# Experts sorted by count on the chip, narrower blocks by rank, and some steps of the first half put elsewhere

## The chip, the cores and the metric

The kernel runs on one core of a Trainium2 chip. The metric is the device time of one execution in microseconds (us): 286.27 us is the median of three runs (285.29, 286.27 and 289.05). The engines are named as in the profile: PE (TensorE matmul; PEld is its weight load), DVE (VectorE), ACT (ScalarE), POOL (GpSimd) and SP (SyncE, which here only issues DMAs). An engine works through its own instructions in the order in which they stand, and waits at the first one whose inputs are not there.

## The reference

Two computations follow each other. The first is a state-space scan (Mamba-2 SSD) over 4 batches, 8 heads, 768 positions, head size 32 and state size 16. The second takes its output as 3072 tokens of width 256 and gives each token to one of 8 experts:

```
logits = xn @ en.T / tau                  # xn, en: tokens and expert embeddings, normalised
expert_idx = argmax(logits, axis=1)       # one expert for a token
gate_w = softmax(logits)[token, expert_idx]
for e in range(8):
    mask = expert_idx == e
    h = maximum(x[mask] @ w1[e], 0)       # 256 -> 1024
    out[mask] = gate_w[mask] * (h @ w2[e])  # 1024 -> 256
```

How many tokens each expert gets follows from the data. The reference, worked through with its own inputs, gives experts 0 to 7 the counts 408, 348, 366, 396, 382, 354, 405 and 413. Of expert 0's tokens 271 lie in the first four of the six position chunks.

## The kernel before, in words

**First half, `mamba`.** The 768 positions are cut into six chunks of 128, and each chunk into two pairs of batches, which makes twelve steps `s`. For a step PE computes `scores` (L493, into the PSUM tiles pgA and pgB), ACT copies them out (g, L509) and POOL masks them (L510; DVE masks some, L507), then PE makes `outputs` (L525 from the passed state T, L534 from the masked scores g and the scaled input xs) in the tile py. ACT copies py to yT (`keep_outputs`, L544), PE turns yT into tokens with their router logits (`tokens`, L583, in the tile pz), and ACT copies these to yt (`keep_tokens`, L594), from where SP writes them to a table `rows` in DRAM (L595). On odd steps PE also makes the chunk's `sums` (L552, in pz) from which DVE updates the state (V, L567, then T, L572). In odd steps V stands on DVE behind ACT's copy yt, since both read the tile pz.

Beside this runs the routing: DVE picks the expert of each token (`pick`, L346 to L355), PE counts ranks (`ranks`, L370), DVE turns a rank into a place in a table (`places`, `one_hots`: oh L386, low L415, hi L420, hv L424; ACT adds its part, hv L430) and PE scatters it there (`table`, L437; DVE adds it up in acc, L446). Decay factors are worked out on DVE; `spread_decays` (PE, L251) and `keep_decays` (ACT, fr, L258) spread them over partitions, `turn_inverse` (PE L239, ACT rT L240) transposes their inverses. All of this is in the order in which the code is written, engine by engine; nothing reorders it.

**Second half, `moe`.** Work is cut into nine jobs. Job 0 is the first 256 tokens of expert 0, which are known before the last chunks are through; job 1 is the rest of expert 0 in a block of 160; jobs 2 to 8 are experts 1 to 7 in blocks of 416. A job gathers its rows from DRAM (POOL, indirect DMA, L765), one DMA for each part of up to 128 rows; 416 is made of 128, 128, 128 and 32. PE transposes the parts (`turn_x`, L808; DVE copies xT, L810), multiplies by w1 (`up`, L818, eight slices f; ACT applies the Relu for even f, L822, DVE for odd f, L824), multiplies by w2 (`down`, L833, two slices j; ACT copies yoT for j = 0, L837, DVE for j = 1, L839) and transposes back (`out`, L847), then ACT and DVE scale by the gate (L853, L851) and POOL scatters the rows to the output (L854), again one indirect DMA a part. The gates come from ACT (squares, L776), POOL (a power, L780) and DVE (L786 to L798). A block is as wide as it is whatever the count, so rows beyond the count are computed for nothing.

Weights of expert 0 come in pieces during `mamba`; those of the other experts are two DMAs of 1 MB each from SP (`load_all_weights`, L181 for w1 and L182 for w2), into three buffers in turn. Experts 1 and 2 are requested before the routing table is complete, since their order is fixed.

If an expert has more than 416 tokens (`CAP`), `left_blocks` (spread over the jobs on DVE) counts the blocks that are left, and `leftover` at the end runs a loop over them: first 24 indirect DMAs of token numbers, then for each block weights, a gather, a whole job and a scatter. Each engine reads the number of blocks into a register (L1025) and skips this if it is zero.

## Time and profile before

| what | value |
|---|---|
| median of the runs (three) | 286.27 us |
| the profiled execution | 287.74 us, its span 286.0 us |
| busy: PE, DVE, ACT, POOL | 259.7, 119.3, 82.1, 102.3 us |
| end of `mamba`, first transposes of job 0 | 74.4 us after the span's start |
| jobs 4 to 7, from one `down` to the next | 24.9 us each |
| granted TensorE clock, mean | 0.98 |

The span is the time from the first to the last instruction of the profiled execution; about 1.7 us lie outside it. The profiled execution is 1.47 us above the median. Starts of instructions are counted from the span's start.

### The profile page before, as it was taken

What the parts mean: (1) busy time and instruction counts of PE and PEld (TensorE: products, weight loads), DVE (VectorE), ACT (ScalarE), POOL (GpSimd) and SP (SyncE); (2) the same over time, 40 slices, a digit from 0 to 9 for tenths busy, and PEclk for the clock granted to TensorE, in tenths of its full rate; (3) what the DMA queues carried; (4) which work ended last, traced back from release to release, by engine and by line L of the source; (5) the groups of instructions that cost most, each with busy time, mean ns of one, the idle gap of its engine ahead of it and who ended that gap; (6) DMA issues with size and microseconds to landing.
All of it is one profiled execution on the core that took longest, in us unless ns stands there. A gap on an engine that the chain in (4) does not pass through costs nothing.

```text
span 286.0 us, 5609 instructions
## 1 busy us (share of the span) xinstructions
PE 259.7 (91%) x2177; PEld 170.1 (59%) x2177; DVE 119.3 (42%) x376; ACT 82.1 (29%) x210; POOL 102.3 (36%) x124
## 2 busy tenths in 40 slices
PE   7698888859998999997999999999999999999980
PEld 6477677747787975554555555555555555555540
DVE  8875888964652431214304223330512323051140
ACT  3644655551421232032122103212220321222130
POOL 7724224443035263055107404710740470114024
PEclk9999999986999999999999999999999999999996
DMA  5656575840597361416224340622530020001001
GB/s 168 213 186 225 184 256 165 256 123 22 192 374 229 123 216 69 147 33 209 54 109 144 112 147 20 219 76 91 157 105 2 19 87 5 0 2 58 0 1 65
DMA packets 21342, 34.79 MB, mean 122 GB/s; under 512 B 2888, under 2 KB 14356, under 8 KB 21312
## 3 DMA queue, kind: packets, MB, share of 16 engines
q1 hardware_dynamic: 18272, 27.94, 29.3%
q0 software_dynamic: 2816, 6.40, 7.2%
q8 instruction: 18, 0.29, 0.4%
q14 instruction: 12, 0.10, 0.1%
q10 hardware_dynamic: 224, 0.06, 0.1%
HBM read 28.26 MB, written 6.65 MB: 122 GB/s over the span
## 4 chain that ended last, share of the span: by engine, by line
PE 52%; issue 22%; DVE 13%; POOL 7%; ACT 4%; POOLq 1%; DVEq 0%
PE bank L818 21%; PE bank L833 20%; POOL out_dram L854 3%; DVE low L415 3%; PE bank L808 2%; PE pz L583 2%; POOL xg L765 2%; PE py L534 2%; PE bank L847 1%; ACT yt L594 1%; PE py L525 1%; POOL g L510 1%; PE pgA L493 1%; ACT yo L853 1%; ACT g L509 1%
## 5 line engine op out<-in xcount | busy, mean ns | idle before, releaser
L818 PE MATMUL bank<-xT,w 128*128 128x416 f32 (+2 forms) x288 | 93.2, 475 | 1.2 <-DVE xT L810 0.8
L833 PE MATMUL bank<-hT,w 128*128 128x416 f32 (+2 forms) x288 | 91.7, 476 | 0.0
L833 PEld LDWEIGHTS bank<-hT,w 128*128 128x128 f32 x288 | 52.5, 190 | 34.9 <-issue 33.7
L818 PEld LDWEIGHTS bank<-xT,w 128*128 128x128 f32 x288 | 52.1, 190 | 35.4 <-issue 32.1
L824 DVE TENSOR_SCALAR hT<-bank 128x416 f32<-128x416 f32 (+2 forms) x33 | 18.3, 553 | 61.4 <-PE bank L818 59.1
L780 POOL TENSOR_TENSOR gr<-gr,half 128x4 f32<-128x4 f32 (+1 forms) x9 | 8.8, 975 | 94.1 <-ACT sq L776 94.1
L854 POOL DMA_INDIRECT out_dram<-yo,to x30 | 29.3, 977 | 23.1 <-ACT yo L853 15.3
L765 POOL DMA_INDIRECT xg<-rows,table x30 | 30.5, 1018 | 19.4 <-DVE to_u L465 11.2
L822 ACT ACTIVATE hT<-bank 128x416 f32<-128x416 f32 (+2 forms) x39 | 18.1, 470 | 62.7 <-PE bank L818 62.7
L510 POOL TENSOR_SCALAR_AFFINE_SELECT g<-g 128x1024 f32<-128x1024 f32 x16 | 18.1, 1144 | 31.5 <-ACT g L509 31.5
L791 DVE TENSOR_SCALAR gr<-gr 128x4 f32<-128x4 f32 (+1 forms) x9 | 1.5, 169 | 59.7 <-POOL gr L780 59.7
L837 ACT COPY yoT<-bank 128x416 f32<-128x416 f32 (+2 forms) x9 | 4.2, 468 | 61.1 <-PE bank L833 61.1
L493 PE MATMUL pgA<-cp,bz 32*128 32x128 f32 x192 | 13.9, 283 | 2.6 <-DVE cp L281 1.4
L534 PE MATMUL py<-g,xs 128*32 128x128 f32 x384 | 15.1, 288 | 0.4 <-issue 0.4
L509 ACT COPY g<-pgB 128x1024 f32<-128x1024 f32 x12 | 12.2, 1017 | 10.2 <-PE pgB L493 7.4
L583 PE MATMUL pz<-turn,yT 128*128 128x136 f32 x88 | 13.9, 304 | 0.9 <-ACT turn L339 0.6
L493 PE MATMUL pgB<-cp,bz 32*128 32x128 f32 x192 | 13.9, 283 | 0.0
L493 PEld LDWEIGHTS pgA<-cp,bz 32*128 32x128 f32 x192 | 11.6, 186 | 3.8 <-DVE cp L281 1.8
L583 PEld LDWEIGHTS pz<-turn,yT 128*128 128x128 f32 x88 | 11.7, 201 | 2.4 <-ACT turn L339 0.7
L534 PEld LDWEIGHTS py<-g,xs 128*32 128x32 f32 x384 | 10.8, 114 | 3.7 <-issue 2.3
L776 ACT ACTIVATE sq<-xg 128x256 f32<-128x256 f32 x32 | 12.9, 408 | 0.0
L847 PE MATMUL bank<-ident,yoT 128*128 128x128 f32 (+1 forms) x64 | 10.1, 276 | 2.9 <-DVE yoT L839 2.0
(200 smaller groups left out, 251.0 us busy)
## 6 DMA issues: line engine op xcount, KB each, us to landing
w<-in_moe_w_dram SPq DMA_DIRECT2D x14, 1024.0 KB, 5.0
rows<-yt SPq DMA_DIRECT2D x12, 264.0 KB, 3.6
in_x<-in_x_dram SPq DMA_DIRECT2D x6, 512.0 KB, 4.8
w<-in_moe_w_dram SPq DMA_DIRECT2D x8, 256.0 KB, 4.3
in_c<-in_CT_dram SPq DMA_DIRECT2D x6, 256.0 KB, 4.2
in_t<-in_B_dram SPq DMA_DIRECT2D x6, 256.0 KB, 5.7
bz<-in_BT_dram SPq DMA_DIRECT2D x40, 32.0 KB, 3.0
xg<-rows,table POOLq DMA_INDIRECT x30
```

The lines of the kernel that those rows point to most:

```text
L493: k.nc.tensor.matmul((k.pgA, k.pgB)[q // 2][:, q % 2, a : a + 128], lhsT=t.bz[r, v, b + i, :], rhs=t.cp[r, b + i, :], start=True, stop=Tru ...
L509: nc.scalar.copy(out=g, in_=ps)
L510: nc.gpsimd.affine_select(out=g, in_=g, pattern=[[0, 8], [1, Q]], compare_op=ALU.is_ge, fill=0.0, base=0, channel_multiplier=-1)
L534: nc.tensor.matmul(k.py[g : g + 32, v, 128 * i : 128 * i + 128], lhsT=t.xs[:, b + i, 4 * v + q, :], rhs=s.g[:, q, 2 * i + v, :], start=(c ...
L583: k.nc.tensor.matmul(at_[:, i, at : at + Y1], lhsT=yT[:, j, i, :], rhs=k.turn[:, j, :], start=(j == 0), stop=(j == 1), skip_group_check=True,)
L765: s.k.nc.gpsimd.indirect_dma_start(out=s.x[0:p, i, 0:TOK], out_offset=None, in_=rows, in_offset=bass.IndirectOffsetOnAxis(ap=s.at[0:p, i : ...
L818: nc.tensor.matmul(t, lhsT=s.w1[:, j, 128 * f : 128 * f + 128], rhs=s.xT[:, j, :], start=(j == 0), stop=(j == KD - 1))
L822: nc.scalar.activation(s.hT[:, f, :], t, ACT.Relu)
L824: nc.vector.tensor_scalar_max(s.hT[:, f, :], t, 0.0)
L833: nc.tensor.matmul(t, lhsT=s.w2[:, f, 128 * j : 128 * j + 128], rhs=s.hT[:, f, :], start=(f == 0), stop=(f == KF - 1))
L847: nc.tensor.transpose(t[:p, 128 * j : 128 * j + 128], s.yT[:, j, o : o + p], k.ident[:])
L854: d = nc.gpsimd.indirect_dma_start(out=k.out[:, :], out_offset=bass.IndirectOffsetOnAxis(ap=s.to[0:p, i : i + 1], axis=0), in_=y[:p], in_o ...
```

## The change

**Experts by rank.** When the table is complete, DVE computes for each of experts 1 to 7 how many experts have a larger key (key = 8 x count + a tie-break; expert 0 gets a key above all). That is its rank r. The table of rows is then permuted so that row block r belongs to the expert of rank r, and `expert[r]` holds its number. Expert 0 stays rank 0. The block of rank r has a fixed width: 416 (expert 0, still 256 + 160), then 416, 408, 400, 384, 368, 356 and 352. The last four need three parts instead of four, so three gathers, three transposes a half and three scatters. With the counts above, the sorted counts of experts 1 to 7 are 413, 405, 396, 382, 366, 354 and 348.

**Weights by register.** SP reads `expert[r]` into a register and addresses the two weight DMAs of rank r with it (`load_sorted`). All of these now come behind the sort; those of ranks 1 and 2 are requested one behind the other.

**Leftover.** Its bound is the width of the expert's rank (`cap`), worked out on DVE by two more instructions beside job 1 and two more in a later job. The step numbers `step` are made on POOL at the start instead of beside job 2.

**Order.** Job 1's `turn_x` stands before job 0's second `down`. In `mamba`: the chunk 0 input for `sums` (in_t) is requested before the eight small DMAs of bz for chunk 1; `turn_embeddings` stands before `outputs`; `spread_decays` with its two copies moves from step 4 to step 5, `turn_inverse` from step 6 to step 7, the second half of `between` (DVE, g_raw and whole, L265 and L269) from step 5 to step 6, and in step 10 the state T is passed before `places` and `one_hots`.

The core of the diff:

```diff
-EARLY, LATE, CAP = 256, 160, 416
+EARLY = 256
+WIDTHS = (416, 416, 408, 400, 384, 368, 356, 352)
+CAP = max(WIDTHS)
...
+    k.slots = ramp("slots", E)
+    k.step_f = ramp("step", LEFT)
+    k.width = c.tile([128, E], F32, name="width")
+    for r, w in enumerate(WIDTHS):
+        nc.gpsimd.memset(k.width[:, r : r + 1], float(w))
...
-def load_all_weights(k, e):
-    w1, w2 = k.wbuf[e % 3]
-    k.w1t[e], k.w2t[e] = w1, w2
-    k.nc.sync.dma_start(w1[:], k.w1[e].rearrange("(k p) f -> p k f", p=128))
-    k.nc.sync.dma_start(w2[:], k.w2[e].rearrange("(f p) m -> p f m", p=128))
+def fetch_weights(k, e, w1, w2):
+    k.nc.sync.dma_start(w1[:], k.w1[bass.ds(e, 1)].rearrange("o (k p) f -> p (o k) f", p=128))
+    k.nc.sync.dma_start(w2[:], k.w2[bass.ds(e, 1)].rearrange("o (f p) m -> p (o f) m", p=128))
+
+
+def load_sorted(k, r):
+    e = k.nc.values_load(k.expert[0:1, r : r + 1], engines=(SP,), min_val=0, max_val=E - 1)
+    fetch_weights(k, e, *k.wbuf[r % 3])
...
+def sort_experts(k):
...
+    v.scalar_tensor_tensor(out=key[:], in0=k.count[:], scalar=float(E), in1=k.order[:], op0=ALU.mult, op1=ALU.add)
+    v.memset(key[:, 0:1], float(E * (T + 1)))
...
+    v.tensor_tensor(out=above[:], in0=bc(key[:], ee, 1), in1=bc(key[:], ee, 2), op=ALU.is_gt)
...
+    v.reduce_sum(out=rank[:], in_=above[:], axis=AX.X)
...
+    v.tensor_tensor(out=at[:], in0=bc(rank[:], ee, 1), in1=bc(k.slots[:], ee, 2), op=ALU.is_equal)
...
+    v.tensor_tensor(out=names[:], in0=at[:], in1=bc(k.slots[:], ee, 1), op=ALU.mult)
...
+        v.reduce_sum(out=k.expert[:], in_=names[:], axis=AX.X)
...
+    v.reduce_sum(out=rows[:], in_=pick[:], axis=AX.X)
+    k.table = k.const.tile([128, E, NT], I32, name="table")
+    v.tensor_scalar_add(k.table[:], rows[:], float(NONE))
...
-    load(k, 1, "cb")
+    load(k, 1, "c")
     load(k, 0, "t")
-    load(k, 1, "xt")
+    load(k, 1, "bxt")
...
+        if s == 2:
+            turn_embeddings(k, k.pz[0])
         outputs(k, s - 1)
...
-        if s == 6:
+        if s == 7:
             turn_inverse(k, 1, k.py[:, 0, 256:384])
         if s % 2 and c < NC - 1:
             sums(k, c)
...
-        if s == 4:
+        if s == 5:
             spread_decays(k, (4, 5))
             keep_decays(k, 4)
             keep_decays(k, 5)
...
     if s == 5:
         inverse(k, 1)
-        next(k.whole_at[1])
-        next(k.whole_at[1])
...
     c = s // 2
+    pass_states(k, c - 1)
     if s == 10:
         places(k, 3)
         one_hots(k, 3)
-    pass_states(k, c - 1)
...
+    if s == 6:
+        next(k.whole_at[1])
+        next(k.whole_at[1])
...
-    k.table = indices(k, "table", 0, E * NT)
-    jobs[1] = Job(k, k.xg[1], [128, 32], k.w1t[0], k.w2t[0], k.table[:, 2:4])
+    late = indices(k, "late", EARLY // 128, NT)
+    w = CAP - EARLY
+    jobs[1] = Job(k, k.xg[1], parts(w), *k.wbuf[0], late[:, 0 : len(parts(w))])
     jobs[1].gather(k.rows[:, :])
...
+    sort_experts(k)
+    jobs[1].to = k.to[:, 0, EARLY // 128 : EARLY // 128 + len(parts(w))]
+    load_sorted(k, 1)
+    load_sorted(k, 2)
...
+            k, k.xg[(r + 1) % 3], parts(WIDTHS[r]), *k.wbuf[r % 3], k.table[:, r], k.to[:, r],
...
     j0.down(0)
     j0.squares()
+    jobs[1].turn_x()
     j0.down(1)
-    jobs[1].turn_x()
...
-    step_i = tile_("step_i", [128, LEFT], I32)
-    nc.gpsimd.iota(step_i[:], pattern=[[1, LEFT]], base=0, channel_multiplier=0)
-    step_f = tile_("step_f", [128, LEFT])
-    nc.vector.tensor_copy(out=step_f[:], in_=step_i[:])
+    step_f = k.step_f
```

Three places show how this moves instructions. Line numbers of the changed kernel differ: its L443, L603, L653, L271 are hv, yT, yt and fr, which are L430, L544, L594 and L258 before. On ACT, from step 4 into step 5, before:

```order
L544 COPY yT<-py 128x512
L258 COPY fr<-py 128x512 x2
L594 COPY yt<-pz 128x264 x2
L509 COPY g<-pgB 128x1024
L509 COPY g<-pgA 128x1024
L430 ACTIVATE hv<-hi,part 128x4x32
L544 COPY yT<-py 128x512
L594 COPY yt<-pz 128x264 x2
```

and now:

```order
L603 COPY yT<-py 128x512
L653 COPY yt<-pz 128x264 x2
L568 COPY g<-pgB 128x1024
L568 COPY g<-pgA 128x1024
L443 ACTIVATE hv<-hi,part 128x4x32
L603 COPY yT<-py 128x512
L271 COPY fr<-py 128x512 x2
L653 COPY yt<-pz 128x264 x2
```

The two copies fr now stand between hv, yT and the copy yt of step 5, not between yT and yt of step 4. The PE transposition of the inverses (L239, now L252) stood on PE in step 6 before that step's tokens:

```order
L525 MATMUL py<-cp,T 32x128 x16
L534 MATMUL py<-g,xs 32x128 x16
L239 MATMUL py<-ident,r 128x64
L583 MATMUL pz<-turn,yT 128x136 x4
L370 LDWEIGHTS before_b
```

and now stands in step 7, between outputs and that step's sums and tokens:

```order
L584 MATMUL py<-cp,T 32x128 x16
L593 MATMUL py<-g,xs 32x128 x16
L252 MATMUL py<-ident,r 128x64
L611 MATMUL pz<-xs,in_t 32x64 x16
L642 MATMUL pz<-turn,yT 128x136 x4
L450 LDWEIGHTS low
```

What moved is one small matmul, ahead of two groups that did not wait for it before. On DVE, between the last addition to the table and job 0's last Relu (hT, slice f = 7), before:

```order
L446 TENSOR_TENSOR acc<-acc,bank_1407 128x64
L452 SCALAR_TENSOR_TENSOR table_f<-acc 128x32
L456 TENSOR_SCALAR table<-table_f 128x32
L465 TENSOR_SCALAR to_u<-table 128x32
L466 TENSOR_SCALAR to_u<-table 128x32
L468 SCALAR_TENSOR_TENSOR to_t<-to_u,table 128x32
L472 SCALAR_TENSOR_TENSOR to<-to_u,to_t 128x32
L824 TENSOR_SCALAR hT<-bank_1402 128x256
```

and the second half of what stands there now:

```order
L493 TENSOR_TENSOR sort_at<-sort_rank,slots 128x64
L496 SCALAR_TENSOR_TENSOR sort_f<-acc 128x32
L500 TENSOR_TENSOR sort_names<-sort_at,slots 128x64
L503 TENSOR_REDUCE sort_expert<-sort_names 128x8
L506 TENSOR_TENSOR sort_pick<-sort_f,sort_at 128x256
L511 TENSOR_REDUCE sort_rows<-sort_pick 128x32
L513 TENSOR_SCALAR table<-sort_rows 128x32
L524 TENSOR_SCALAR to_u<-table 128x32
L525 TENSOR_SCALAR to_u<-table 128x32
L527 SCALAR_TENSOR_TENSOR to_t<-to_u,table 128x32
L531 SCALAR_TENSOR_TENSOR to<-to_u,to_t 128x32
L883 TENSOR_SCALAR hT<-bank_1417 128x256
```

Between acc and sort_at stand seven more: two for job 1's rows (`late`) and five of the sort (two for the key, its memset, above and rank). The Relu hT, which had six instructions ahead of it, has eighteen.

## The prediction

> **What bounds the kernel now.** I read the windows by stage first (columns: stretch, its length, busy time of PE, PEld, DVE, ACT and POOL, granted clock, DMA share, GB/s).

> ```profile
> 40.00:62.00 22.00, 18.77 (x541) 16.17 (x539) 18.59 (x59) 12.71 (x23) 8.66 (x8) 1.00 0.65 204
> ...
> 75.00:90.00 15.00, 14.62 (x80) 12.66 (x81) 7.08 (x39) 4.47 (x15) 5.97 (x7) 1.00 0.97 342
> 183.00:208.00 25.00, 24.87 (x82) 13.90 (x81) 7.01 (x19) 5.32 (x16) 9.14 (x9) 1.00 0.36 116
> ```

> From 75 us on PE is the bound: 24.87 of 25 us, with DVE at 7. Up to 75 us PE and DVE are both nearly full and wait for each other in turn. So the second half is costed by PE time, the first by who waits for whom. The chain of waits shows one expert (start, length, work), then job 1's `down` at width 160:

> ```profile
> 141.79 11.37 PE bank L833 x32
> 153.16 2.79 PE bank L818 x8
> ...
> 157.14 8.38 PE bank L818 x24
> 165.52 1.16 PE bank L808 x8
> ```
> ```profile
> 98.07 4.54 PE bank L833 x32
> ```

> **Widths.** `down` takes 11.37 us at 416 columns and 4.54 at 160, 26.7 ns a column, and `up` at 416 takes 2.79 + 8.38 = 11.17, nearly the same. Twice 26.7 is 53.4 ns a column for both; by proportion it is (11.37 + 11.17)/416 = 54.2. Ranks 1 to 7 hold 2684 columns where seven times 416 were 2912: 228 fewer, 12.2 to 12.4 us. I take **-12.2**. A width of 352 costs some 300 ns a multiplication (11.37/32 x 352/416), well above 160's 142, so it lies between two measured widths.

> **Fourth parts.** Four blocks have three parts. `turn_x` has 8 transposes for 1.16 us; six at 0.145 give 0.87: -0.3 each. `out` fills the time from 153.16 + 2.79 to 157.14, 1.19 for eight, 0.88 for six: -0.3, in three blocks (the fourth is the tail). Together 7 x 0.29 = **-2.0**.

> **Tail.**

> ```profile
> 270.66 0.51 ACT L837 COPY yoT<-bank 128x416 f32<-128x416 f32 x1 [6.47 <-PE bank L833]
> 276.33 0.58 DVE L839 COPY yoT<-bank 128x416 f32<-128x416 f32 x1
> 280.73 0.97 POOL L854 DMA_INDIRECT out_dram<-yo,to  x1 [0.30 <-issue]
> ```

> A scatter takes POOL 0.97 us and 0.30 ahead of it, and the last four follow each other without a pause; three instead of four: -1.3. Against it, the last yoT on DVE comes 5.67 us after that on ACT, behind the gates and the last piece of `left_blocks`. Without the fourth square (0.40) and with smaller copies this is 5.2, while the last `down` slice shrinks to 11.37/2 x 352/416 = 4.8: 0.4 of the width's gain is lost. **-0.9**.

> **Step numbers and job 1's transposes.**

> ```profile
> 129.84 0.18 DVE L964 CAST step_f<-step_i 128x32 f32<-128x32 int32 x1 [3.85 <-POOL step_i L962]
> 130.97 1.29 PE L847 MATMUL bank<-ident,yoT 128*128 128x128 f32 x7 [1.31 <-DVE yoT L839]
> ```
> ```profile
> 74.39 0.60 PE L808 MATMUL bank<-ident,xg 128*128 128x128 f32 x4
> 83.27 7.07 PE L833 MATMUL bank<-hT,w 128*128 128x256 f32 x32
> ...
> 91.86 1.35 PE L818 MATMUL bank<-xT,w 128*128 128x160 f32 x8 [0.81 <-DVE xT L810]
> ```

> DVE stood 3.85 us behind POOL's step numbers, which stood behind four gathers, and yoT and PE behind it: **-1.3**. On POOL twelve small instructions for the new constants, at most about 0.2 us each as L964 is on DVE, fall into a wait of 2.55 us for ACT, which is cover for them:

> ```profile
> 17.11 1.09 POOL L510 TENSOR_SCALAR_AFFINE_SELECT g<-g 128x1024 f32<-128x1024 f32 x1 [2.55 <-ACT g L509]
> ```

> The 0.81 us for which PE waits for job 1's xT goes, since half a `down` (3.5 us) covers the copy: **-0.8**. But the transposes now come half a `down` sooner, at 86.8, and need job 1's rows:

> ```profile
> 70.31 1.00 POOL L765 DMA_INDIRECT xg<-rows,early_i  x1 [0.30 <-issue]
> 82.49 1.00 POOL L765 DMA_INDIRECT xg<-rows,table  x1 [11.18 <-DVE to_u L465]
> 83.80 0.94 POOL L765 DMA_INDIRECT xg<-rows,table  x1 [0.30 <-issue]
> ```

> Issued by 84.74, they have 2.1 us. The early gather was issued by 71.31 and read without a wait at 74.39, so a landing takes at most 3.1 us: cost 0 to 1.0, with `down` queued behind. I take 0, as the weights that fill the DMA engines here (share 0.97) now come later.

> **The sort** stands on DVE ahead of job 0's last Relu.

> ```profile
> 82.47 0.24 DVE L468 SCALAR_TENSOR_TENSOR to_t<-to_u,table 128x32 f32<-128x32 int32 x1
> 82.75 0.19 DVE L472 SCALAR_TENSOR_TENSOR to<-to_u,to_t 128x32 int32<-128x32 int32 x1
> 83.47 0.42 DVE L824 TENSOR_SCALAR hT<-bank 128x256 f32<-128x256 f32 x1 [0.53 <-PE bank L818]
> ```

> Twelve instructions more: ten small ones, 0.19 long and at most 0.28 apart (82.47 to 82.75), and two of 0.42 over 256 elements a row, as the Relu is: 2.7 to 3.6 us. The chain that ended at 82.94 ends at 85.6 to 86.5, the Relu at 86.1 to 87.0. The first `down` slice (half of 7.07 us from 83.3) needs it for its last eighth, at 86.4. Cost 0 to 0.6; I take **+0.2**, as not all of the ten hang on the one before. These instructions run beside POOL's gathers. L468 ran beside the gather at 82.49 in 0.24 us. [...]

> The number of the rank-1 expert is there after eleven of the eighteen, by 84.9 at 0.28 each from 81.8.

> ```profile
> L1025 SPq TENSOR_LOAD <-left_table x1: 472/472/472, 276.4 to 276.4; - x1
> ```
> ```profile
> DMA to landing us min/median/max: 4.8/5.0/5.8
> ```

> SP's register load takes 0.47. A 1 MB transfer of w1 lands 4.8 to 5.8 us after its issue (second row), so by 92 with 1 us for the rest of the issue. PE needs it after job 1's `down`, which ends at 98.07 + 4.54 = 102.6: ten us to spare. Behind SP's wait stand only the weights of later ranks.

> **First half.** The rows of SP's queue, then of PE, DVE and ACT:

> ```profile
> 5.86 4.18 SPq L154 DMA_DIRECT2D bz<-in_BT_dram  x8
> 10.09 0.42 SPq L160 DMA_DIRECT2D in_t<-in_B_dram  x1
> ```

> ```profile
> 14.13 0.65 PE L552 MATMUL pz<-xs,in_t 128*32 128x64 f32 x32 [1.58 <-DMA in_t<-in_B_dram]
> 28.04 1.16 PE L251 MATMUL py<-f,spread 32*128 32x128 f32 x16 [0.98 <-DVE f L225]
> ...
> 43.25 0.63 PE L552 MATMUL pz<-xs,in_t 128*32 128x64 f32 x32
> 43.81 1.19 PE L583 MATMUL pz<-turn,yT 128*128 128x136 f32 x8
> 64.45 1.11 PE L525 MATMUL py<-cp,T 32*32 32x128 f32 x32 [3.40 <-DVE T L572]
> ```
> ```profile
> 30.91 0.19 DVE L386 TENSOR_TENSOR oh<-pz,ob 128x32 f32<-128x32 f32 x1 [0.42 <-ACT yt L594]
> 36.07 0.42 DVE L567 TENSOR_TENSOR V<-T,pz 128x256 f32<-128x256 f32 x1 [0.58 <-ACT yt L594]
> ...
> 38.77 0.30 DVE L265 TENSOR_TENSOR g_raw<-fr 128x8 f32<-128x8 f32 x1
> ...
> 39.38 1.22 DVE L507 TENSOR_TENSOR g<-pgA,mask 128x1024 f32<-128x1024 f32 x1
> ...
> 47.08 0.42 DVE L567 TENSOR_TENSOR V<-T,pz 128x256 f32<-128x256 f32 x1 [0.57 <-ACT yt L594]
> ```
> ```profile
> 29.23 1.07 ACT L258 COPY fr<-py 128x512 f32<-128x512 f32 x2 [2.59 <-PE py L251]
> 45.92 0.57 ACT L544 COPY yT<-py 128x512 f32<-128x512 f32 x1
> ```

> in_t is issued at 5.9 instead of 10.09; with the 4.0 us that it took to 14.13 it lands by 10, before sums wants it (12.55). The bz come 0.43 later, the last issued at 10.5, and scores of step 2 now wants them at 13.2: with 2.7 us against in_t's 4.0 they may be up to 1.3 late. I take the gain whole, and keep the loss as an end: -1.6 up to step 4. Without L251 in step 4, oh (30.91) gains the 0.42 that it waited for yt beyond DVE's own work: -2.0. In step 5 the moved L251 (1.16) and fr (1.07) stand between yT and yt, for which V waits at 36.07: +2.3, so V comes 0.3 late. DVE's g_raw and whole, gone from step 5, give back the 0.6 from 38.77 to 39.38: -0.3. In step 6 they fall into DVE's wait of 0.57 before 47.08. In step 7, L239 must wait for yT (46.49) as both use py, and sums (0.6) and tokens (1.2), done at 45.0 before, wait behind it: L239 0.25 + 0.6 + 1.2 puts yt and V back by 2.05: +1.75. From here to the end of the scan DVE is nearly full (18.59 of 22 us), so I let all of it go through. The earlier T saves 0.35, as the scaled xs behind it on DVE still comes after `one_hots`: +1.4.

> PE then stands idle from 43.0 (where sums began, 0.3 sooner) to 46.2, some 3.1 us. What that does to the clock:

> ```profile
> 64.00:66.00 2.00, 1.55 (x44) 1.16 (x48) 2.00 (x3) 0.08 (x1) 0.00 (x0) 0.50 0.03 8
> ```

> After the 3.40 us of idle time before 64.45 the clock stood at a half. If 3.1 us do the same, the 2.05 us of PE work in step 7 take 1.3 more and the first half costs **+2.7**; if not, +1.4. I take +2.7, as 3.1 is near the 3.40 seen. [...] Ends: -2.0, if both moved matmuls find ACT done, and +4.3, if in_t's 1.6 is not gained either.

> **Sum.** -12.2 - 2.0 - 0.9 - 1.3 - 0.8 + 0.2 + 2.7 = -14.3. The profiled execution (287.74, span 286.0) would take 273.4; it lies 1.47 above the median of 286.27, so on the runs **272.0 us**.

> **Rivals.**
> - *The clock stays full in step 7*: PE's 3.1 us of idle time are less than the 3.40 that the trace shows before a half clock, and may be too short. 272.0 - 1.3 = 270.7. Chance 0.2. [...]
> - *The first half gains*: the moved matmuls cost nothing, 272.0 - 4.7 = 267.3. Against it stand the waits at 36.07 and 47.08; a DVE that is slower than I reckon would hide them. 0.18.
> - *Covers fail at the seam*: job 1's rows or the last Relu come late, up to 1.5: 273.5. 0.09.
> - *The first sorted weights come late*: all 4 MB and a job's gather are requested at once after 85 us. Nothing speaks for it but that 75 to 90 us ran at a share of 0.97; they would have to take 17 us instead of 12 (4.2 MB at 342 GB/s) for 276. 0.07.
> - *Narrow blocks don't pay*, if a fixed cost a multiplication hid between 160 and 416: half of 12.2 gone, 278. The two slopes speak against it. 0.05.
> - *Slower: an expert has more tokens than its rank's width.* One token too many starts `leftover`: 24 indirect DMAs at 1.27 us (30 us), then a block one step after the other: weights (5.8), gather and landing (4), `up` and `down` at 128 columns (twice 4.54 x 0.8), gates and scatter (7): some 24 us. About 326. The counts worked out from the reference leave 2 to 4 columns a rank, so it needs another routing on the chip. 0.03.

> The forecast itself has 0.38. **Range** 266.5 to 276: it leaves out the two last rivals and an edge of the first-half and weights cases, under 2 in 10. A measurement of this kernel tells about 2% (5.7 us) from no change, 280.5 here: faster 0.94, same 0.03, slower 0.03.

> **What would show it.** `down` at 352 near 9.6 us and 54 ns a column; jobs of three parts with six transposes; no wait of DVE on step numbers; V behind yt in step 7 later than the V of step 5 by 12 to 13 us instead of 11.0, with PE idle about 3 us before L252; the rank-1 weights landed ten us before use. It is wrong if the first transposes of job 0 start before 74.4, if PE waits for weights at the first ranked job, or if the loop of `leftover` runs.

## The result, and the profile after

The changed kernel takes **271.0 us** (median of four runs, 269.66 to 272.65), where the kernel before took 286.79 us in the runs beside it: a ratio of 0.9446, with a 95% interval of 0.9362 to 0.953. Six more runs, taken later, gave a median of 271.02 us and a ratio of 0.9393 (0.9352 to 0.9434). The forecast was 272.0 us, in a range of 266.5 to 276.

The profiled execution took 269.66 us, its span is 267.9 us. Set beside the profile before (span 286.0), and cut at four points that both have, the span shows where the time went:

| stretch | before, us | after, us | difference | predicted |
|---|---|---|---|---|
| start to the first transposes of job 0 | 74.39 | 76.11 | +1.72 | +2.7 |
| to the first `up` of rank 1 | 28.06 | 27.21 | -0.85 | -0.6 |
| ranks 1 to 7, to the end of the last `down` | 173.77 | 155.62 | -18.15 | -15.5 |
| to the end of the span | 9.78 | 8.96 | -0.82 | -0.9 |
| sum | 286.0 | 267.9 | -18.1 | -14.3 |

The ranked jobs are where it was earned. First PE's order of time in the kernel before (each line: start, length, engine, line of the kernel, operation, tiles, shapes, count, and in brackets how long the engine stood idle before it and for whom), for one job of 416 columns, from `turn_x` to the next one's `down`:

```profile
240.00 1.32 PE L808 MATMUL bank<-ident,xg 128*128 128x128 f32 x8
241.25 11.44 PE L833 MATMUL bank<-hT,w 128*128 128x416 f32 x32
252.52 2.96 PE L818 MATMUL bank<-xT,w 128*128 128x416 f32 x8
255.32 1.34 PE L847 MATMUL bank<-ident,yoT 128*128 128x128 f32 x8
256.49 8.55 PE L818 MATMUL bank<-xT,w 128*128 128x416 f32 x24
264.88 11.34 PE L833 MATMUL bank<-hT,w 128*128 128x416 f32 x32
```

Then the same view of the changed kernel: `turn_x` of three parts, the whole of the narrowest job, and at the top the seam.

```profile
76.11 0.60 PE L867 MATMUL bank<-ident,xg 128*128 128x128 f32 x4
...
84.99 3.62 PE L892 MATMUL bank<-hT,w 128*128 128x256 f32 x16
88.45 0.88 PE L867 MATMUL bank<-ident,xg 128*128 128x128 f32 x4
...
103.32 2.96 PE L877 MATMUL bank<-xT,w 128*128 128x416 f32 x8
...
163.79 0.82 PE L867 MATMUL bank<-ident,xg 128*128 128x128 f32 x6
164.45 10.91 PE L892 MATMUL bank<-hT,w 128*128 128x400 f32 x32
...
239.18 2.53 PE L877 MATMUL bank<-xT,w 128*128 128x352 f32 x8
241.55 0.82 PE L906 MATMUL bank<-ident,yoT 128*128 128x128 f32 x6
242.21 7.26 PE L877 MATMUL bank<-xT,w 128*128 128x352 f32 x24
249.31 9.63 PE L892 MATMUL bank<-hT,w 128*128 128x352 f32 x32
258.78 0.27 PE L906 MATMUL bank<-ident,yoT 128*128 128x128 f32 x1
```

Lengths in such rows overlap a little, so starts are subtracted. `up` and `down` at 416 columns take (252.52 - 241.25) + (255.32 - 252.52) + (264.88 - 256.49) = 22.46 us, at 352 columns 2.37 + 7.10 + 9.47 = 18.94: 55.0 ns a column, 12.5 us for 228 columns. `turn_x` of four parts takes 1.25, of three 0.66; `out` 1.17 and 0.66. Four of the one and three of the other make 3.9 us. The wait for step numbers is worth 1.5 (the start of `out` to what follows was 2.70 us there, 1.17 elsewhere). Together 17.9 of the 18.15.

The seam holds. Job 1's transposes at 88.45 follow half a `down` without a wait. On DVE the sort ends with the last small operation on `to` and the Relu follows without a gap; SP requests the first sorted weights 17 us before rank 1 starts at 103.32, and a transfer of 1 MB lands after 5.2 us (median of the issues there). The changed kernel's DVE and SP in order of time:

```profile
87.24 0.19 DVE L531 SCALAR_TENSOR_TENSOR to<-to_u,to_t 128x32 int32<-128x32 int32 x1
87.35 0.42 DVE L883 TENSOR_SCALAR hT<-bank 128x256 f32<-128x256 f32 x1
```
```profile
86.59 0.40 SPq L189 DMA_DIRECT2D w<-in_moe_w_dram  x1
```

In the first half the waits that were foreseen are there. In the same order of time, the V of steps 3, 5 and 7 on DVE (the first operation of the state update, which stands behind ACT's copy yt) and what PE waits for at the two moved steps, the spread (L264) and the inverse's transpose (L252):

```profile
22.21 0.42 DVE L626 TENSOR_TENSOR V<-T,pz 128x256 f32<-128x256 f32 x1 [2.74 <-ACT yt L653]
36.08 0.42 DVE L626 TENSOR_TENSOR V<-T,pz 128x256 f32<-128x256 f32 x1 [2.91 <-ACT yt L653]
50.02 0.42 DVE L626 TENSOR_TENSOR V<-T,pz 128x256 f32<-128x256 f32 x1 [3.08 <-ACT yt L653]
```
```profile
33.20 1.16 PE L264 MATMUL py<-f,spread 32*128 32x128 f32 x16 [1.51 <-ACT yT L603]
45.74 0.37 PE L252 MATMUL py<-ident,r 64*128 64x64 f32 x1 [2.21 <-ACT yT L603]
```

V of steps 5 and 7 stood on yt for 0.58 and 0.57 us before; now it stands 2.9 and 3.1.

### The profile page after: what moved, and what is told of

It reads as the page before. It is cut to its first block, busy times and chain, and to the rows that moved or that the text cites. A ratio compares the mean times of both kernels' runs of the same rounds, so it can differ in the third digit from the quotient of the medians.

```text
span 267.9 us, 5605 instructions
## 1 busy us (share of the span) xinstructions
PE 244.6 (91%) x2161; PEld 169.8 (63%) x2161; DVE 118.9 (44%) x387; ACT 79.7 (30%) x202; POOL 95.1 (35%) x127
## 4 chain that ended last, share of the span: by engine, by line
PE 61%; issue 15%; DVE 12%; DMA 4%; ACT 3%; POOL 2%; SPq 1%; POOLq 1%; DVEq 0%
PE bank L877 24%; PE bank L892 24%; PE pz L642 3%; DVE low L428 2%; PE bank L867 2%; DVE g L566 2%; PE py L593 2%; DVE xs L303 2%; POOL out_dram L913 2%; DMA in_x<-in_x_dram 2%; PE bank L906 1%; ACT yt L653 1%; DMA w<-in_moe_w_dram 1%; DMA out_dram<-yo,to 1%; PE py L584 1%
## 5 line engine op out<-in xcount | busy, mean ns | idle before, releaser
L877 PE MATMUL bank<-xT,w 128*128 128x256 f32 (+8 forms) x288 | 87.0, 454 | 0.4 <-ACT yt L653 0.4
L892 PE MATMUL bank<-hT,w 128*128 128x256 f32 (+8 forms) x288 | 85.5, 455 | 0.0
L883 DVE TENSOR_SCALAR hT<-bank 128x160 f32<-128x160 f32 (+8 forms) x33 | 17.3, 524 | 56.6 <-PE bank L877 56.6
L839 POOL TENSOR_TENSOR gr<-gr,half 128x3 f32<-128x3 f32 (+2 forms) x9 | 8.1, 904 | 83.2 <-ACT sq L835 83.2
L913 POOL DMA_INDIRECT out_dram<-yo,to x26 | 25.7, 990 | 23.5 <-ACT yo L912 17.7
L881 ACT ACTIVATE hT<-bank 128x256 f32<-128x256 f32 (+8 forms) x39 | 17.3, 450 | 56.2 <-PE bank L877 56.2
L824 POOL DMA_INDIRECT xg<-rows,table x24 | 24.9, 1035 | 7.5 <-issue 5.0
L896 ACT COPY yoT<-bank 128x256 f32<-128x256 f32 (+8 forms) x9 | 4.0, 446 | 54.7 <-PE bank L892 50.7
L593 PE MATMUL py<-g,xs 128*32 128x128 f32 x384 | 14.5, 288 | 5.1 <-DVE xs L303 3.5
L552 PE MATMUL pgA<-cp,bz 32*128 32x128 f32 x192 | 14.1, 286 | 2.2 <-DVE g L566 1.9
L593 PEld LDWEIGHTS py<-g,xs 128*32 128x32 f32 x384 | 10.5, 114 | 8.3 <-DVE xs L303 3.8
L642 PE MATMUL pz<-turn,yT 128*128 128x136 f32 x88 | 15.1, 321 | 0.3 <-DVE acc L459 0.3
L568 ACT COPY g<-pgB 128x1024 f32<-128x1024 f32 x12 | 12.2, 1013 | 8.8 <-PE pgB L552 7.2
L552 PE MATMUL pgB<-cp,bz 32*128 32x128 f32 x192 | 14.1, 286 | 0.0
L642 PEld LDWEIGHTS pz<-turn,yT 128*128 128x128 f32 x88 | 12.7, 215 | 2.3 <-issue 1.1
L552 PEld LDWEIGHTS pgA<-cp,bz 32*128 32x128 f32 x192 | 11.7, 187 | 3.4 <-DVE g L566 2.4
L552 PEld LDWEIGHTS pgB<-cp,bz 32*128 32x128 f32 x192 | 11.7, 187 | 0.0
L835 ACT ACTIVATE sq<-xg 128x256 f32<-128x256 f32 x28 | 11.3, 409 | 0.0
## 6 DMA issues: line engine op xcount, KB each, us to landing
rows<-yt SPq DMA_DIRECT2D x12, 264.0 KB, 3.3
```

The lines of the kernel that those rows point to most:

```text
L552: k.nc.tensor.matmul((k.pgA, k.pgB)[q // 2][:, q % 2, a : a + 128], lhsT=t.bz[r, v, b + i, :], rhs=t.cp[r, b + i, :], start=True, stop=Tru ...
L568: nc.scalar.copy(out=g, in_=ps)
L593: nc.tensor.matmul(k.py[g : g + 32, v, 128 * i : 128 * i + 128], lhsT=t.xs[:, b + i, 4 * v + q, :], rhs=s.g[:, q, 2 * i + v, :], start=(c ...
L642: k.nc.tensor.matmul(at_[:, i, at : at + Y1], lhsT=yT[:, j, i, :], rhs=k.turn[:, j, :], start=(j == 0), stop=(j == 1), skip_group_check=True,)
L824: s.k.nc.gpsimd.indirect_dma_start(out=s.x[0:p, i, 0:TOK], out_offset=None, in_=rows, in_offset=bass.IndirectOffsetOnAxis(ap=s.at[0:p, i : ...
L835: nc.scalar.activation(sq[:], s.x[:, i].rearrange("p (j w) -> p j w", j=2)[:, :, 0:128], ACT.Square, accum_out=s.r[:, i : i + 1],)
```

## The experiments

Times are medians; each set of runs had its own runs of the kernel before (medians of 286.8 to 288.1 us), so the ratio to these, with its interval, is the safer figure. In all diffs the line taken out is the changed kernel's, unless it is said that a kernel starts from the one with both steps back (of the second group).

**Even widths.**

```diff
-WIDTHS = (416, 416, 408, 400, 384, 368, 356, 352)
+WIDTHS = (416,) * 8
```

> The changed kernel with eight widths of 416 in place of the falling ones; the sort, the order by count, the register loads and the first half stay. Theory A, the rows of the two profiles: 12.7 us for 228 columns, 4.1 for the fourth parts (0.62 for the transposes ahead of up and 0.52 for those of the output, for each block), 0.8 at the end: 17.6 over 271.0, about 288.6, which is over the kernel before. Rival B, the sizes of the prediction (12.2 + 2.0 + 0.9): 286.1, as the kernel before. Rival C, the sort's order itself gains or costs, and the widths little: 280 or less.

287.68 us, ratio 1.0008 (0.9968 to 1.0047). With even widths the rest of the change (sort, register loads, seam, step numbers, first half) is worth nothing as a whole. Theory C falls. The time lies between those of theories A and B, so the profile has to decide. In it job 0 starts at 77.65 us of a span of 286.7, so its second half takes 209.05 us, 17.25 more than the changed kernel's 191.8 (267.9 - 76.11): the sizes of theory A (17.6) rather than those of the prediction (15.1). Against the kernel before (286.0 - 74.39 = 211.6) the even kernel's second half is 2.55 shorter, the step numbers and the seam; its first half gives that back.

**The first half: all moves back, one back, both back.**

With all moves back the loads are as before, and the embeddings' transpose, the last states and the second half of `between` stand where they stood, as do the two steps of the next diff:

```diff
-    load(k, 1, "c")
+    load(k, 1, "cb")
...
-    load(k, 1, "bxt")
+    load(k, 1, "xt")
```

Of this one the next two kernels have the first change (the inverse) or the second (the spread), and the fourth has both:

```diff
-        if s == 7:
+        if s == 6:
             turn_inverse(k, 1, k.py[:, 0, 256:384])
...
-        if s == 5:
+        if s == 4:
             spread_decays(k, (4, 5))
```

> The changed kernel with every move in the first half undone (in_t, the spread of the last decays, the second inverse's transpose, the whole products, the embeddings' transpose and the last states stand where they stood before); widths, sort and seam stay as changed. Theory A, as predicted: the moves together cost. Job 0's first transposes, 76.11 us in the changed kernel's profile against 74.39 before, come at 74.4 again, and the time falls by 1.7 (the two profiles) to 2.7 (the sum of the prediction), to 268.3 to 269.3. Rival B, the moves are even or gain, and the later start in the one profile is scatter between executions: 271 or above.

> The changed kernel with the second inverse's transpose alone back in step 6. Theory A: its wait for yT holds sums and tokens in step 7, so the V of step 7 follows that of step 5 by 11.0 to 11.5 us instead of 13.94, PE's 2.21 us of idle time ahead of the transpose and the half clock behind it go, and 2.5 to 2.9 us reach the end: about 268.3. Rival B: DVE is nearly full there and beside POOL, so it is what is late next, V comes 1 us sooner at most and the end moves by less than 0.7.

> The changed kernel with the spread of the last decays alone back in step 4. Theory A: L264 (1.16) and fr (1.07) no longer stand between yT and yt in step 5, while oh of step 4 waits 0.42 for yt again: the V of step 5 comes 1.7 to 1.9 sooner, and the end as much, about 269.2. Rival B: step 4 loses what step 5 gains, since the one-hots wait for yt there; the end moves by less than 0.5.

> The changed kernel with both of these back, in_t, the last states, the whole products and the embeddings' transpose left as changed. Theory A: the two add up, 4.2 to 4.7 sooner, about 266.5, which is under the kernel with all moves undone, since the early in_t (1.6) and the early last states stay. Rival B: no more than the larger of the two alone.

| kernel | median, us | ratio (95%) | V of step 3 to 5, us | V of step 5 to 7, us |
|---|---|---|---|---|
| before | 286.8 to 288.1 | 1 | 12.12 | 11.01 |
| changed | 271.0 | 0.9446 (0.9362 to 0.953) | 13.87 | 13.94 |
| all moves back | 269.72 | 0.941 (0.9353 to 0.9466) | 12.11 | 11.01 |
| inverse back in step 6 | 267.69 | 0.9326 (0.9283 to 0.9368) | 14.32 | 11.38 |
| spread back in step 4 | 268.44 | 0.9368 (0.9318 to 0.9418) | 12.54 | 11.86 |
| both back | 266.14 | 0.9277 (0.9225 to 0.9329) | 12.82 | 10.23 |

The two right columns come from DVE's order of time, of the kernel before (its V of steps 5 and 7 stand in the prediction), of that with all moves back, with the inverse back, with the spread back (its V of step 3 starts at 22.21, as in the changed kernel), and with both:

```profile
23.95 0.42 DVE L567 TENSOR_TENSOR V<-T,pz 128x256 f32<-128x256 f32 x1 [3.26 <-ACT yt L594]
```
```profile
26.12 0.42 DVE L626 TENSOR_TENSOR V<-T,pz 128x256 f32<-128x256 f32 x1 [4.05 <-ACT yt L653]
38.23 0.42 DVE L626 TENSOR_TENSOR V<-T,pz 128x256 f32<-128x256 f32 x1 [0.57 <-ACT yt L653]
49.24 0.42 DVE L626 TENSOR_TENSOR V<-T,pz 128x256 f32<-128x256 f32 x1 [0.57 <-ACT yt L653]
```
```profile
22.64 0.42 DVE L626 TENSOR_TENSOR V<-T,pz 128x256 f32<-128x256 f32 x1 [2.74 <-ACT yt L653]
36.96 0.42 DVE L626 TENSOR_TENSOR V<-T,pz 128x256 f32<-128x256 f32 x1 [3.36 <-ACT yt L653]
48.34 0.42 DVE L626 TENSOR_TENSOR V<-T,pz 128x256 f32<-128x256 f32 x1
```
```profile
34.75 0.42 DVE L626 TENSOR_TENSOR V<-T,pz 128x256 f32<-128x256 f32 x1 [0.57 <-ACT yt L653]
46.61 0.42 DVE L626 TENSOR_TENSOR V<-T,pz 128x256 f32<-128x256 f32 x1 [1.62 <-ACT yt L653]
```
```profile
22.48 0.42 DVE L626 TENSOR_TENSOR V<-T,pz 128x256 f32<-128x256 f32 x1 [2.74 <-ACT yt L653]
35.30 0.42 DVE L626 TENSOR_TENSOR V<-T,pz 128x256 f32<-128x256 f32 x1 [0.57 <-ACT yt L653]
45.53 0.42 DVE L626 TENSOR_TENSOR V<-T,pz 128x256 f32<-128x256 f32 x1
```

V's wait for yt in step 5 is 2.9 to 3.4 us wherever the spread stands in step 5 and 0.5 to 0.6 wherever it doesn't; in step 7 it is 1.6 to 3.1 us wherever the inverse stands in step 7, and at most 0.57 where it is back. So theory A's mechanism holds for both. Between the V rows the spread costs 1.3 to 1.5 us, less than the expected 1.7 to 1.9, and the inverse 1.6 to 2.6. In time the two together cost 4.9 us against the changed kernel's first runs and, by the ratios, 3.3 against its six later ones (0.9393, below). Each alone costs 2.2 to 3.4 by the ratio to the first runs and 0.7 to 1.9 to the later ones, but there the intervals overlap, so the price of one move is shown by the V rows rather than by the time. The profiles also differ by where the half clock falls, on which more below. With both back the time lies 3.6 us under the kernel with all moves back. All of that is there at the V of step 3 already (22.48 against 26.12): the early in_t, for which PE waits 2.08 us with all moves back, and a half clock from 15 to 19 us that no other profile of the table has there.

One thing is left open. The kernel with all moves back missed its expected 268.3 to 269.3 us, and its interval overlaps that of the changed kernel, so by itself it does not show that the moves cost. It has steps of the same length as the kernel before (12.11 and 11.01 us), yet by the difference of the second halves (211.6 - 191.8 = 19.8) it should take some 267 us and takes 269.72. Besides that half clock its profile shows job 0 waiting 0.37 us for its rows; whether all its runs have these isn't shown.

**The same program again.** The changed kernel, unaltered.

> The changed kernel once more, for a second profile of the same program. The kernels that share its first half word for word, or all but one step of it, had the half clock in different places (35 to 39, 45.5 to 49 and 69 to 73 us in the changed kernel; none but 66 to 70 where only the spread was back, 35.5 to 43 and 66 to 73.5 or 63 to 70.5 alone in two kernels with equal first halves). Theory A: the clock falls by windows of some 3.5 us that run on by themselves, so the same idle stretches meet them differently each time: the waits of PE are the same again within 0.2 us, the half-clock stretches lie elsewhere or are fewer, and the median is 270 to 272. Rival B, the prediction's term: an idle stretch of a given length brings the half clock always, so the stretches behind step 5, step 7 and step 10 stand in the same places.

Median 271.02; the profiled run took 271.99, with a span of 270.3 and job 0 at 78.44 us. Its second half is 191.86 us where the first profile has 191.79, so all that differs between these two executions differs in the first half. The windows by stage (length, busy time of PE, PEld, DVE, ACT, POOL, granted clock, DMA share, GB/s) of the first profile, of the second, and of the kernel with the spread back:

```profile
34.00:41.00 7.00, 6.28 (x129) 4.91 (x129) 4.69 (x13) 3.88 (x8) 2.04 (x2) 0.76 0.54 146
45.50:52.50 7.00, 6.76 (x145) 5.84 (x146) 3.70 (x15) 2.43 (x6) 1.10 (x2) 0.76 0.43 125
```
```profile
34.00:41.00 7.00, 5.33 (x129) 4.53 (x129) 3.86 (x12) 4.32 (x10) 2.05 (x2) 1.00 0.52 164
45.50:52.50 7.00, 5.46 (x117) 4.72 (x121) 4.47 (x17) 2.37 (x7) 1.53 (x2) 0.76 0.33 99
```
```profile
41.00:49.00 8.00, 5.79 (x169) 4.78 (x158) 6.09 (x21) 4.37 (x9) 3.07 (x3) 1.00 0.63 205
```

PE waits 2.21 us ahead of the inverse's transpose in all three (the order of time of the second profile and of the kernel with the spread back; the second profile puts the wait down to a transfer of bz, which this matmul doesn't read, but in all three it starts 3.29 us behind the start of L593 ahead of it):

```profile
47.04 0.27 PE L252 MATMUL py<-ident,r 64*128 64x64 f32 x1 [2.21 <-DMA bz<-in_BT_dram]
```
```profile
43.79 0.27 PE L252 MATMUL py<-ident,r 64*128 64x64 f32 x1 [2.21 <-ACT yT L603]
```

Behind the same wait the clock fell in two executions and not in the third, and the half clock of 35 to 39 us in the first profile isn't in the second. Theory B falls.

```profile
42.17:45.58 3.41, 1.36 (x59) 0.89 (x40) 3.23 (x11) 2.70 (x4) 2.14 (x2) 1.00 0.90 309
```
```profile
42.44:45.85 3.41, 2.06 (x49) 1.84 (x49) 2.47 (x8) 1.09 (x3) 1.33 (x2) 1.00 0.79 266
```

PE was busy for 1.36 us of the one, and the clock fell; for 2.06 of the other, and it stayed full. So theory A holds: what counts, as far as these traces show, is how much of a window PE works, and the same wait falls into the windows differently in each execution.

**The early in_t.** From the kernel with both steps back:

```diff
-    load(k, 1, "c")
+    load(k, 1, "cb")
     load(k, 0, "t")
-    load(k, 1, "bxt")
+    load(k, 1, "xt")
```

> The kernel with both steps back (266.1 us), and the loads of the second chunk too in the order they had before, so that in_t comes after all eight bz. Theory A: what the early in_t gains (1.6 us up to step 3) is lost again a step later. In the four kernels with the early in_t PE stands 1.2 to 1.6 us in step 3 at the same matmul (the 24th of 32 of L593), with no releaser but the issue of instructions, and starts again at 25.1 to 25.7 us, about 2.3 us after a 16 KB packet of PE's instruction queue; where in_t was late PE reaches that matmul after that time. Then the order of the loads is worth nothing: 265.8 to 266.8, with V of step 3 1.6 later and no wait of 1 us or more on instructions. Rival B, the prediction's term: the early in_t is worth its 1.6, and this kernel takes 267.7 or more.

268.33 us, ratio 0.9323 (0.9287 to 0.9359) against 0.9277 (0.9225 to 0.9329). The V of step 3 comes 1.42 us later (23.90 against 22.48), that of step 5 still 1.25 later, and the time is 2.2 longer, with intervals that overlap; in the profiles 1.2 us come behind the V of step 9, where this one has 6.8 us of half clock and the one with the early in_t 3.4. Theory A falls: the gain is not given back, and the wait for instructions stands here too, with in_t late.

```profile
26.97 0.49 PE L593 MATMUL py<-g,xs 128*32 128x128 f32 x9 [1.32 <-issue]
```

**The fourth part.** Two kernels, both from both steps back; the first transposes a short part as a whole one, the second gives the output's fourth part another bank (a bank is a piece of PSUM that PE writes to).

```diff
-                nc.tensor.transpose(t[:, o : o + p], s.x[0:p, i, Y1 * j : Y1 * j + 128], k.ident[:p, :p])
+                h = 128 if p <= 64 else p
+                nc.tensor.transpose(t[:, o : o + h], s.x[0:h, i, Y1 * j : Y1 * j + 128], k.ident[:h, :h])
```
```diff
-            t = k.bank["ot"]()
+            t = k.bank["yp" if i == 3 else "ot"]()
```

> The kernel with both steps back, and the last part of a block, where it has 32 rows or fewer, is transposed ahead of up as a whole part of 128 rows (the rows behind it are old ones, and their columns aren't read). Theory A: the two transposes of such a part cost 0.31 us each against 0.11 of a whole one, because the load of a part of another height waits 0.17 for the PE to run empty, not because there is one part more; the four blocks with such a part (job 1 and three ranks) save 0.4 each: 1.6, about 264.5, and the eight transposes take 0.85 to 0.9 from start to start of what follows instead of 1.25. Rival B: the cost is that of a fourth part as such (bank, copy), and nothing changes: 266.1.

> The kernel with both steps back, and the output's transposes of a fourth part go to a bank of the down ring, as the three banks of their own ring are taken. Theory A: the fourth part waits 0.36 us for ACT's yo of the first, since it uses its bank again; the three blocks with a fourth part save 0.3 to 0.36 each, about 1.0: 265.1. Rival B: the short parts' height costs it, as ahead of up, and nothing changes: 266.1.

Whole parts: 264.94 us, ratio 0.9221 (0.9186 to 0.9256). Another bank: 266.26 us, ratio 0.9269 (0.9222 to 0.9316). PE's order of time, first with whole parts, then with the other bank:

```profile
112.98 1.04 PE L868 MATMUL bank<-ident,xg 128*128 128x128 f32 x8
113.85 11.34 PE L893 MATMUL bank<-hT,w 128*128 128x416 f32 x32
```
```profile
127.13 1.04 PE L906 MATMUL bank<-ident,yoT 128*128 128x128 f32 x8
128.01 8.39 PE L877 MATMUL bank<-xT,w 128*128 128x408 f32 x24
```

`turn_x` of eight whole transposes takes 0.87 us from start to start, not 1.24: theory A holds in that a part of 32 rows is dearer than one of 128. The `down` behind it takes 11.18 us (from 113.85 to the next `up` at 125.03), not 11.27 as with both steps back, so the short part costs 0.1 us there too; four blocks at 0.37 + 0.1 are 1.9. `out` takes 0.88, not 1.17, so there the price is the wait for the bank, as theory A has it, though the median doesn't show it. From job 1's transposes to the end of the span the kernel with both steps back takes 264.0 - 84.48 = 179.5 us, with whole parts 265.1 - 87.36 = 177.7, with the bank 264.0 - 85.39 = 178.6: 1.8 and 0.9 less. The 0.9 is smaller than the scatter of the time (265.25 to 269.44 us in six runs), and the 1.2 us that whole parts gain in time have intervals that overlap; both gains are shown by their stage.

**x ahead of the one-hots in step 10**, from both steps back:

```diff
-    if s == 10:
-        places(k, 3)
-        one_hots(k, 3)
     scale_x(k, c)
+    if s == 10:
+        places(k, 3)
+        one_hots(k, 3)
```

> The kernel with both steps back (266.1 us), and DVE scales x for step 10 ahead of the one-hots of that step, not behind them. Theory A: PE's wait of 3.5 us at L593 for xs, which every kernel so far has, is work of DVE that others have put in front (places, low, hi, hv, some 3.4 us); xs is done 3.2 us sooner, and hv, 1.2 later, is what L450 waits for next, from 62.1 to 64.3 us instead of 65.8: 1.5 sooner, and 0.7 to 1.3 more where the clock no longer falls to a half behind that wait. 263.3 to 264.6. Rival B: the wait goes to L450 whole, since low grows beside POOL, and the end moves by less than 0.7.

264.28 us, ratio 0.9196 (0.9156 to 0.9235). PE's order of time in step 10 with both steps back, and now:

```profile
64.23 1.66 PE L593 MATMUL py<-g,xs 128*32 128x128 f32 x32 [3.50 <-DVE xs L303]
```
```profile
62.72 0.28 PE L450 MATMUL pz<-hv,low 128*128 128x64 bf16 x4 [1.47 <-ACT hv L443]
63.88 2.18 PE L642 MATMUL pz<-turn,yT 128*128 128x136 f32 x8 [0.88 <-DVE acc L459]
```

The wait of 3.5 us is gone (L593 starts at 60.17, right behind L584), and two of 1.47 and 0.88 are there instead, at the place that theory A named: 1.9 us of time, in the range that it gave, with intervals that just overlap. The clock still fell to a half there, from 63.9 to 67.3 us, where theory A had it full.

**All together, and bz later.** Both steps back, x first, whole parts, the fourth bank; the second kernel also requests the fourth chunk's bz in step 3:

```diff
-            load(k, s // 2 + 2, "cb")
+            load(k, s // 2 + 2, "c" if s == 2 else "cb")
...
+        if s == 3:
+            load(k, 3, "b")
```

> Both steps back, x first in step 10, whole parts ahead of up, and a bank of the down ring for the fourth part of the output. Theory A: the parts add up, from 266.1: 1.6 for whole parts, 1.0 for the bank, 1.5 to 2.8 for x: 260.7 to 262.0. Rival B: the bank is worth nothing in the time, as its run alone had it (266.26), and x nothing: 264.5.

> As the kernel with all of these, and the eight bz of the fourth chunk (wanted in step 6) are requested in step 3 instead of step 2. Theory A: PE's wait of 1.2 to 1.5 us for the issue of instructions in step 3 comes from a code packet that stands behind data while the DMA engines are full (share 0.9 to 1.0 from 20 to 23.5 us); with half of the data gone there the wait is under 0.5 and the V of step 5 comes about 1 us sooner. Rival B: the packet is asked for only when PE has used up the code before, so that the wait stays over 1 us whatever else is on the DMA engines.

All together: **262.62 us**, ratio 0.9096 (0.9046 to 0.9145), less than any kernel above and 8.4 us less than the changed one. The median misses theory A's range (260.7 to 262.0) by 0.6, which its interval reaches, and theory B's time by more: by themselves the parts had given 4.9 and 1.9 in time and 1.8 and 0.9 in their stage, 9.5 together, so they add up nearly, not wholly. Its profiled execution ran at half clock for 6.8 us from 27 to 34 us; whether the others did isn't shown. With bz later 262.4 us, ratio 0.912 (0.9083 to 0.9157): no difference. The wait for instructions in step 3 is still there, 1.18 us at 25.14, but the DMA share from 20 to 23.5 us fell from 0.96 to 0.88 only, since other transfers came sooner in place of bz. So the wait stays over 1 us as theory B has it, but this run does not decide between the two theories.

## Why the prediction was right

Widths, fourth parts, tail and step numbers were to carry the gain, the first half to cost some of it, and sort and weights to hide; that is what the table at the top and the experiments show. Point by point:

- **Widths**: 12.2 predicted, 12.5 measured, 55.0 ns a column against 53.4 to 54.2. Of the 22.46 us at 416 columns 0.1 belong to the short part, as the run with whole parts shows; without it the price is 53.4 ns. `down` at 352 takes 9.63 us.
- **Fourth parts**: 2.0 predicted, 3.9 measured. This term was mis-sized. I priced a part by proportion, 0.29 us, where it costs 0.59 ahead of `up` (and 0.1 more in the `down` behind) and 0.51 in `out`. A part of 32 rows is not a quarter of the work of four: its two transposes cost about 0.30 us each where a whole one costs 0.11, and in `out` the fourth part waits for one of three banks. The runs with whole parts and with a fourth bank show each by itself. The rows to see it by were there: two parts of 128 took 0.60 us at 74.39, and a part of 128 with one of 32 took 0.88 at 90.17.
- **Tail**: 0.9 and 0.82; DVE's last yoT comes 5.05 us behind ACT's (254.24 and 259.29), where I had 5.2.
- **Step numbers** 1.3 and 1.5. **Job 1's transposes and the sort** -0.6 and -0.85: the rows were there in time, and the last Relu ended at 87.77 us, 11.66 behind the first transposes where it was to be 11.7 to 12.6, and didn't hold PE.
- **Weights by register**: hidden, with some ten us to spare.
- **First half**: +2.7 predicted, +1.72 and +4.05 in the two profiles. Its parts: in_t 1.6 predicted, 1.74 at the V of step 3 (22.21 against 23.95) in the first profile, 0.38 in the second (23.57), which has a half clock from 10.5 to 14.5 us; the spread 1.9 between the V of steps 3 and 5, 1.75 in the profiles; the inverse 2.05 without the clock and 3.35 with it, 2.94 and 2.06 in the two profiles. The 0.3 of g_raw and whole didn't come: DVE's g of step 5 starts at 39.47 where it was 39.38, since ob, beside a mask on POOL, took 0.81 us. The early last states were to save 0.35, which the runs don't show: from the V of step 9 to job 0 it is 17.21 us (all moves back) and 18.61 (the kernel before) with them late, and 16.69 to 18.79 with them early, in the nine profiles in which step 10 is as in the changed kernel.
- **The half clock in step 7** was the wrong step in the sum. PE stood idle 2.21 us ahead of L252, not 3.1, and the clock fell in two of three executions all the same. I made the clock a function of the length of one idle stretch; the runs show it isn't. The 1.3 us for it had no working: from L252 to the hv matmul L450 it is 1.81 us at full clock (the kernel with the spread back), and 3.27 and 2.33 in the changed kernel's two profiles, so the half clock cost 1.5 and 0.5. A rival had the clock stay full, since 3.1 us were less than the 3.40 that the trace before shows ahead of a half clock: that a shorter stretch leaves the clock alone is not borne out, though its 270.7 us happens to lie near the result. With windows that run on by themselves the traces agree, by the whole multiples of 3.413 us above.

The forecast lies 1.0 us from the measured median, closer than its terms deserve, and that is luck: 2.7 us too little for the ranked jobs, and on the median up to 1.3 us too little cost in the first half, for by the second halves (19.8 us less) and the medians (15.8 to 17.1 less) that costs 2.7 to 4.0 us. The two errors take away from each other. The profiles differ by more (18.1 us) than the medians, as that of the kernel before lay above its median and that of the changed one below.

## What to carry to other kernels

Price a remainder by its own rows, not by proportion: here a last part of 32 rows cost 0.59 us ahead of `up`, where a whole one costs 0.22, since it has another height than the parts beside it, and 0.51 in `out`, as the one too many for a ring of three banks. A step that was moved later on one engine delayed what that engine had queued behind it (V came 1.3 to 1.5 us later by the spread and 1.6 to 2.6 by the inverse), and it is worth undoing each move by itself, since here two of them gave away 3.3 to 4.9 us inside a change that gained some 16. When a stage's own length repeats to 0.1 us and the total scatters by 3, judge an edit in its stage.

## What the runs showed of the hardware

**Some DVE instructions took longer beside POOL's masks.** The four `low` of a step take 0.73 us with POOL idle (at 77.20 in the changed kernel) and up to 2.46 beside its masks (at 55.27). In the changed kernel's order of time the DVE instruction ends where POOL's ends, within 0.15 us, for POOL's two masks from 43.44 to 45.73 and its one from 37.11 to 38.20:

```profile
37.11 1.09 POOL L569 TENSOR_SCALAR_AFFINE_SELECT g<-g 128x1024 f32<-128x1024 f32 x1 [5.11 <-ACT g L568]
37.44 0.81 DVE L365 TENSOR_TENSOR ob<-oh,m 128x32 bf16<-128x32 f32 x1
...
43.44 2.29 POOL L569 TENSOR_SCALAR_AFFINE_SELECT g<-g 128x1024 f32<-128x1024 f32 x2 [4.29 <-ACT g L568]
44.81 1.06 DVE L437 TENSOR_TENSOR hv<-hi,vals 128x128 bf16<-128x128 f32 x1
```

An hv with no mask beside it (at 32.28) takes 0.29 us. Why these take longer there isn't shown. The prediction has the sort run beside POOL's gathers; there it wasn't seen: beside the gather at 84.17 to 85.16 the sort's instructions of two inputs took 0.22 to 0.23 us, and none lasted as long as the gather.

**A part of another height.** Ahead of the transpose of a part of 32 rows the weight load waits 0.17 us with no releaser (PEld in the changed kernel's order of time), once for each of the two (at 98.04 and 98.69, for rank 1):

```profile
98.69 0.14 PEld L867 LDWEIGHTS bank<-ident,xg 32*128 32x128 f32 x1 [0.17 <-issue]
```

Where the part is transposed whole the eight transposes take 0.87 us from start to start, not 1.24, so the cost goes with the height. What the weight load waits for isn't shown; that it is for PE to run empty was my guess in theory A.

**PE waits for its instructions.** In twelve of the thirteen profiles of the changed kernel and its variants (all but the one with all moves back) PE stands 0.6 to 2.0 us at the same place, nine matmuls ahead of the end of `outputs` of step 3, for nothing but issue; in all twelve a packet of 16 KB on a queue for instructions ends 1.2 to 1.5 us before it goes on (2.2 to 2.8 from the packet's start), so the wait is most likely for that packet. The changed kernel, whose packet came from 23.25 to 24.25 us:

```profile
25.57 0.52 PE L593 MATMUL py<-g,xs 128*32 128x128 f32 x9 [1.61 <-issue]
```

The kernel before has no such wait there. The page of the changed kernel counts 17 packets on that queue, and no other wait for issue in its PE's order of time is over 0.24 us. Why PE waits for this packet stays open: neither the later in_t nor the later bz took it away. With all moves back PE comes to this `outputs` only at 27.02 us, 1.25 behind the end of its packet (25.77), which fits with there being no wait.

**Half-clock stretches** were one or two windows of 3.41 us long in every profile that has them, and three kernels with word-for-word the same first half had them at 64.5 to 68, at 35.5 to 43 and 66 to 73.5, and at 63 to 70.5 us (read in steps of half a us). With PE the bound behind them, as from step 10 to job 0, 3.4 us more of it make the same work 1.9 us longer: from the V of step 9 to job 0 it took 16.69 us in the first profile of the changed kernel (half clock from 69 to 73) and 18.60 in the second (68.5 to 76).
